# Second ranking placed behind the turns of its step, one product a block sooner, row copies on ScalarE, stores and first weights at other slots

## The chip, the cores and the metric

The kernel runs on one core of a Trainium2 chip. The core has five engines, each with its own instruction queue worked through in order: TensorE (PE, matmuls; its weight loads are shown apart as PEld), VectorE (DVE), ScalarE (ACT), GpSimd (POOL) and SyncE (SP), which here only issues transfers. They wait for one another through semaphores. Transfers between memory and the core are issued from SP or POOL and run on 16 DMA engines.

The metric is the device time of one launch in microseconds (us); smaller is better. Several runs are given by their median.

## The reference

Sigmoid attention for 8 batches of 12 heads, 448 tokens of width 64; its heads, put side by side, are rows of 768; then in each batch the 128 rows with the highest gate score go through a two-layer network and are added back.

```python
def _attn_ref(q, k, v):            # q, k, v: (8, 12, 448, 64)
    scores = 1.0 / np.sqrt(64) * np.matmul(q, k.transpose(0, 1, 3, 2)) - np.log(448)
    attn = 1.0 / (1.0 + np.exp(-scores))
    return np.matmul(attn, v)

def _moe_ref(x, w_gate, w1, w2, capacity):   # x: (8, 448, 768), w1: 768 x 1024, capacity 128
    scores = np.einsum('bsd,d->bs', x, w_gate)
    out = x.copy()
    for b in range(8):
        top_idx = np.argpartition(-scores[b], capacity)[:capacity]
        xe = x[b, top_idx]
        ye = np.maximum(xe @ w1, 0.0) @ w2
        g = 1.0 / (1.0 + np.exp(-scores[b, top_idx]))
        out[b, top_idx] = x[b, top_idx] + g[:, None] * ye
    return out
```

## The kernel before

**Steps and slots.** The heads are taken in 24 quads of four, two quads to a step: 12 steps `s`, of 7 slots `n` each. A batch is three quads. In a slot PE makes scores for a piece of the keys (`score`, L338) into the PSUM banks `PA`, ACT turns them into weights (`squash`, L352), and PE multiplies earlier weights with values (`value`, L367) into four output banks `PO`. Outputs of step s−1 are complete in slot 3 of step s. There DVE transposes them out (`takes`, L388) into the batch's tile `x_b`, of which there are two.

**Order by hand.** The whole program is one written order; each engine runs its share in that order. `slot(s, n)` issues the attention work and `after(s, n)` all else at that place. In slot 3 from step 4 on, `block(s)` adds work of the network, listed in `BLOCKS`: `("c", b)` chooses the rows of batch b, `("t", b)` turns the gathered rows, and `(m, p, key)` is product `key` of matrix m for the pair of batches p. Products are those of a seven-product scheme for two by two blocks: the two batches of a pair are combined, and so are quarters of the matrices, so the weights need sums of quarters.

**From output to chosen rows.** `gates` multiplies the outputs with the gate vector and adds up (L396, L399). When a batch is complete, `gate` forms its scores, and POOL writes them to memory (L424). `spread` reads them back onto all partitions as `rep` (L436, POOL queue). `ranking(b)` counts on DVE, in eight instructions over `rep` (L444, L447), how many tokens stand above each, and `place` makes a mask `hot` of it (L457, L459). `RANKED` gives the slot of each ranking: batch 0 at (3, 1), batch 1 at (4, 1). In a block, `choose(b)` takes the rows' numbers with small matmuls (L481 or L485) into a bank, `fetch` reads them from there on DVE (L492, L495), and POOL gathers the rows from memory (L505) into `xe`, one of three buffers. If the choice is the first item of a block, it stands ahead of the output transposes, and its fetch among them:

```python
        if work and work[0][0] == "c":
            chosen = choose(work[0][1], places.pop(0))
        takes(s - 1, 0)
        if work and work[0][0] == "c":
            fetch(*chosen)
            work = work[1:]
        takes(s - 1, 1)
```

**Turning and adding back.** `turn_rows` transposes the gathered rows on PE into two banks (L523). ACT copies the first half (L525), DVE the second (L526), for the products of the first matrix (`first`, L559). Products of the second (`second`, L623) are added into `xe` by DVE (`second_sums`, L634). After its last addition POOL scatters a batch's rows back (L643), which frees the row buffer.

**Weights.** Both matrices are loaded in quarters by SP, at the slots in `WEIGHTS` (L180). DVE makes sums of quarters (L207) at the slots in `MADE`; `KEPT` says when SP writes a sum to memory (L213), and `LENT` when it is read back (L241). Sums live in three spare tiles.

**SP's queue.** SP holds, in the written order, the loads of queries, keys (L104) and values (L153), the weights and sums, and the stores: `store` (L405) writes a quarter of a batch's rows in pieces of 128 bytes, four stores for each batch. A key load waits until DVE has turned the key tile before it (`turn`, L320); only one raw key tile exists. `FULL` is the step in whose slot 3 a batch is completed: 2, 3, 5, 6, 8, 9, 11, 12.

Of the kernel before, what the change touches and what calls it, by code (L numbers as in the profile page):

```python
# [12 lines left out]
ALU = mybir.AluOpType  # L13
# [4 lines left out]
def kernel(  # L18
# [90 lines left out]
    def spare(n):  # L109
        return spares.tile([P, QW], F32, name=f"spare{n}")  # L110
# [82 lines left out]
    def make_sum(m, key):  # L193
        if key == 5:
            room["a"] = spare(0)
        elif (m, key) == (1, 6):
            room["c"] = spare(2)
        elif m == 2 and key in (4, 6):
            room["d" if key == 4 else "c"] = spare(key // 4 if key == 4 else 0)
        a, b, c, d = [room.get(x) for x in "abcd"]  # L200
        w00, wx, w11 = [(w1_sb, w2_sb)[m - 1][:, x] for x in range(3)]
        dst, x, y, op = {
            (1, 5): (a, b, w11, ALU.add), (1, 7): (b, w00, b, ALU.subtract),
            (1, 6): (c, w11, b, ALU.subtract), (1, 3): (c, wx, c, ALU.subtract),
            (2, 5): (a, b, w00, ALU.subtract), (2, 7): (b, b, w11, ALU.subtract),
            (2, 6): (c, w00, b, ALU.subtract), (2, 4): (d, wx, c, ALU.subtract)}[m, key]
        nc.vector.tensor_tensor(out=dst, in0=x, in1=y, op=op)  # L207
        sums[m, key] = dst
        lent[m, key] = [dst[:, pr * QW // 2:(pr + 1) * QW // 2] for pr in range(2)]

    def keep_sum(m, key):
# [2 lines left out]
        sums[m, key] = t  # L214


    MADE = {(4, 4): (1, 5), (4, 5): (1, 7), (4, 6): (1, 6), (6, 4): (1, 3),
            (6, 6): (2, 5), (7, 0): (2, 7), (7, 4): (2, 6), (7, 5): (2, 4)}
    KEPT = {(4, 5): (1, 5), (4, 6): (1, 7), (5, 1): (1, 6), (6, 5): (1, 3),
            (7, 0): (2, 5), (7, 1): (2, 7), (7, 5): (2, 6), (7, 6): (2, 4)}  # L220
    WEIGHTS = {(2, 6): (1, 0), (3, 1): (1, 1), (3, 2): (1, 2), (3, 4): (1, None),
               (4, 1): (2, 0), (5, 1): (2, 1), (5, 2): (2, 2), (6, 4): (2, None)}

    def attn_tile(pr, n):
        return attnp.tile([P, 2, S], F32, name=f"attn{pr}_{n}")
# [285 lines left out]
    def turn_rows(b, both):  # L511


        n = CAP
        p, odd = divmod(b, 2)
        if not odd:
            t = moe.tile([P, 6 * KH * P], F32, name="rows_t")
            pairs[p] = {"x": t.rearrange("p (m k n) -> p m k n", m=6, k=KH)}
        x = pairs[p]["x"]
        ps = [t.rearrange("p (k n) -> p k n", n=P) for t in both]  # L520
        for t in range(KD):
            a, i = divmod(t, KH)
            nc.tensor.transpose(ps[a][:, i, :n], st[b]["xe"][:n, t * P:(t + 1) * P],  # L523
                                iden[:n, :n])
        nc.scalar.activation(x[:, 2 * odd, :, :n], ps[0][:, :KH, :n], AF.Copy)  # L525
        nc.vector.tensor_copy(x[:, 2 * odd + 1, :, :n], ps[1][:, :KH, :n])  # L526
        st[b]["gate"] = moe.tile([P, 1], F32, name="gate", bufs=4)
        nc.scalar.activation(st[b]["gate"][:n], st[b]["picked"][:n], AF.Sigmoid)
        if not odd:
            return  # L530
        for dst, y, z in ((4, 2, 0), (5, 3, 4), (2, 3, 2)):
            nc.vector.tensor_tensor(out=x[:, dst, :, :n], in0=x[:, y, :, :n],
                                    in1=x[:, z, :, :n], op=ALU.subtract)
        pairs[p]["turned"] = True
        last_row(p)
# [105 lines left out]
    def scatter(b):  # L641
# [37 lines left out]
    def block(s):  # L679

        places = [PA[1][:, 0], PO[0][0], PO[0][1], PA[0][:, 0], PO[1][0], PO[1][1], PA[0][:, 0]]
        work = BLOCKS.get(s, ())
# [4 lines that stand above are left out]
            fetch(*chosen)  # L687
            work = work[1:]
        takes(s - 1, 1)
        if s in FULL:  # L690
            gates(2 * s - 2)
        for item in work:
            if item[0] == "t":
                turn_rows(item[1], [places.pop(0) for _ in range(2)])
            elif item[0] == "c":
                fetch(*choose(item[1], places.pop(0)))
            else:
                finish(item, begin(item, places.pop(0)))
# [83 lines left out]
    def rest():  # L782
# [54 lines left out]
        for key in (1, 2, 6, 5, 3, 7, 4):  # L837
            do((2, p, key))

    def after(s, n):  # L840

        if n == NF and s:
            odd = s in FULL[1::2]
            if s > 4:
                load_v(s)
            if s in BLOCKS:
                block(s)
            elif s in FULL:
                gates(2 * s - 2)
            if odd and s > 3:  # L850
                gates(2 * s - 1)
            turn("q", 2 * s + 2)
            turn("k", 2 * s + 3)
            load("k", 2 * s + 4)
            turn("q", 2 * s + 3)
            if s not in FULL:
                gates(2 * s - 2)
            if not odd or s == 3:
                gates(2 * s - 1)
        for m, key, place in LENT.get((s, n), ()):  # L860
            lend(m, key, place)
        if s == 0:
            if n == 0:
                turn("k", 1)
                turn("q", 1)
                load("k", 2, 3)
                load("q", 2, 3)
            if n == 4:
                turn("k", 2, 3)
                load_v(1)  # L870
                load("k", 4)
            if n == 5:
                turn("q", 2, 3)
        if n == NF + 1 and 0 < s < 4:
            load_v(s + 1)
        if (s, n) in WEIGHTS:
            m, x = WEIGHTS[s, n]
            if x is None:
                load_left(m)
            else:  # L880
                load_held(m, x)
        if (s, n) in KEPT:
            keep_sum(*KEPT[s, n])
        if (s, n) in MADE:
            make_sum(*MADE[s, n])
        for b in range(B - 1):
            full = FULL[b]
            if (s, n) == ((4, 0) if b == 1 else (full, 5 + b % 2)):
                spread(b)
            for a, at in enumerate(((full, 5), (full, 6), (full + 1, 1), (full + 1, 2))):  # L890
                if (s, n) == (at if b < B - 2 else (full, 4 + a // 2)):
                    store(b, (a,))
            if (s, n) == RANKED[b]:
                ranking(b)

    RANKED = [(3, 1), (4, 1), (6, 1), (7, 5), (9, 1), (10, 5), (11, 6)]

    first_outs = ExitStack()

# [58 lines left out]
```

## Time and profile before

| | |
|---|---|
| median of 3 runs | 479.14 us (478.22 to 481.59) |
| profiled execution, its own time | 481.73 us |
| its span, from first to last instruction | 479.9 us |
| PE busy | 447.5 us, 93% |
| VectorE busy | 306.2 us, 64% |
| ScalarE busy | 188.2 us, 39% |
| GpSimd busy | 33.1 us, 7% |
| hardware DMA queue of SP | 67.97 MB, 55.7% of 16 engines |
| one slot of attention, squash to squash, undisturbed | 3.02 us |

The profile is of one execution. A row of a group or of a stretch of time gives line, engine, operation and tiles as output<-inputs. In a list in order of time the two first numbers are the start and the duration in us, and the bracket at the end is the idle time of the engine before the instruction and what ended it. A row of waits gives who waited, for whom, the total in us, how often and the longest. The row PEclk is the granted clock of PE in tenths of full speed, in 40 equal slices of the span; 9 is 90% or more.

### The profile page before, as it was taken

To read this page: it belongs to the slowest core of one execution; us is meant where nothing else is said; L and a number is where in the kernel's file an instruction comes from. 1 tells how busy PE (TensorE), PEld (TensorE's weight loads), DVE (VectorE), ACT (ScalarE), POOL (GpSimd) and SP (SyncE) were. 2 spreads that over 40 slices of the span, in tenths; PEclk is the share of its full clock that TensorE was granted. 3 is DMA by queue.
4 is the path that set the end of the run, shared out by engine and by line. 5 is a ranking of instruction groups with operands and counts; after the bars stand their busy time and mean duration, and the time that the engine had idled before them with its cause. 6 is when DMAs were issued, how large, how long until landed. Compare 5 with 4: busy or idle time off the path is not lost.

```text
span 479.9 us, 14338 instructions
## 1 busy us (share of the span) xinstructions
PE 447.5 (93%) x6374; PEld 267.4 (56%) x6374; DVE 306.2 (64%) x647; ACT 188.2 (39%) x249; POOL 33.1 (7%) x55
## 2 busy tenths in 40 slices
PE   8999997991997999999999599999999999999994
PEld 3556552441335549546556445854655756868952
DVE  4308195755936785865799377571695787886271
ACT  3776664661362462462362165156046250101000
POOL 6000010000001000100000300010000100101001
PEclk9999999997799999999999799999999999999999
DMA  8854318999898295189764378439894786711001
GB/s 231 239 156 110 125 17 171 285 222 243 200 319 237 66 196 107 36 240 289 192 222 117 102 213 188 96 63 280 191 296 135 152 194 162 126 41 72 1 0 66
DMA packets 112846, 76.80 MB, mean 160 GB/s; under 512 B 90304, under 2 KB 99136, under 8 KB 112784
## 3 DMA queue, kind: packets, MB, share of 16 engines
q1 hardware_dynamic: 110800, 67.97, 55.7%
q0 software_dynamic: 1984, 7.91, 5.8%
q8 instruction: 50, 0.82, 0.7%
q14 instruction: 12, 0.10, 0.1%
HBM read 55.41 MB, written 20.46 MB: 158 GB/s over the span
## 4 chain that ended last, share of the span: by engine, by line
PE 83%; DMA 6%; DVE 5%; issue 2%; ACT 2%; SPq 0%; POOLq 0%; DVEq 0%; ACTq 0%
PE a L338 27%; PE o L367 24%; PE o L623 10%; PE o L559 9%; PE a L559 7%; PE a L623 4%; DMA raw_k<-in_k_dram 1%; DMA rep<-scores 1%; ACT attn L352 1%; PE p L914 1%; DMA scores<-total 1%; DVE x_b L388 1%; DMA raw_v<-in_v_dram 1%; DMA xe<-out_dram,idx 1%; ACT hidden L352 1%
## 5 line engine op out<-in xcount | busy, mean ns | idle before, releaser
L338 PE MATMUL a<-qT,kT 32*64 32x448 f32 x2624 | 252.7, 546 | 14.0 <-DVE got L495 10.6
L352 ACT ACTIVATE attn<-a,bias_s 128x896 f32<-128x896 f32 x162 | 161.9, 1007 | 118.5 <-PE a L338 113.0
L367 PE MATMUL o<-attn,raw_v 32*64 32x448 f32 x2176 | 205.0, 546 | 0.7 <-DMA raw_v<-in_v_dram 0.4
L338 PEld LDWEIGHTS a<-qT,kT 32*64 32x64 f32 x2624 | 98.2, 133 | 106.7 <-ACT attn L352 53.8
L367 PEld LDWEIGHTS o<-attn,raw_v 32*64 32x64 f32 x2176 | 79.6, 133 | 38.3 <-issue 27.8
L388 DVE STREAM_TRANSPOSE x_b<-o 128x448 f32<-128x448 f32 x48 | 27.6, 622 | 54.9 <-PE o L367 42.9
L367 PE MATMUL o<-attn,rows_t 32*64 32x448 f32 x448 | 41.9, 537 | 0.0
L320 DVE STREAM_TRANSPOSE kT<-raw_k 128x448 f32<-128x448 f32 x42 | 24.2, 613 | 23.9 <-DMA raw_k<-in_k_dram 20.7
L575 ACT ACTIVATE hidden<-hidden 128x512 f32<-128x512 f32 x12 | 7.5, 630 | 68.5 <-DVE hidden L572 68.5
L399 DVE TENSOR_REDUCE gate_p<-scr 128x14 f32<-128x448 f32 x48 | 29.8, 621 | 1.7
L396 DVE TENSOR_TENSOR scr<-x_b,wg_b 128x448 f32<-128x448 f32 x48 | 29.3, 611 | 1.0
L559 PE MATMUL o<-rows_t,w_sb 128*128 128x128 f32 x192 | 24.4, 287 | 3.4 <-DVE rows_t L526 3.4
L623 PE MATMUL o<-w_sb,hidden 128*128 128x384 f32 x80 | 27.3, 486 | 0.0
L312 DVE STREAM_TRANSPOSE qT<-qT 128x896 f32<-128x896 f32 x23 | 25.0, 1088 | 2.8 <-DMA qT<-in_q_dram 2.7
L444 DVE TENSOR_SCALAR_CACHE_REDUCE scr<-rep,who 128x448 f32<-128x448 f32 (+1 forms) x32 | 21.5, 673 | 6.8 <-DMA rep<-scores 5.9
L559 PEld LDWEIGHTS o<-rows_t,w_sb 128*128 128x128 f32 x192 | 23.7, 203 | 3.8 <-DVE rows_t L526 3.6
L572 DVE TENSOR_TENSOR hidden<-o,hidden 128x512 f32<-128x512 f32 x19 | 12.6, 687 | 19.9 <-PE o L559 19.8
L634 DVE SCALAR_TENSOR_TENSOR xe<-o,gate,xe 128x384 f32<-128x384 f32 x34 | 19.5, 611 | 8.9 <-PE o L623 8.7
L447 DVE SCALAR_TENSOR_TENSOR scr<-rep,who,earlier 128x448 f32<-128x448 f32 (+1 forms) x32 | 21.9, 683 | 1.4
L525 ACT ACTIVATE rows_t<-o 128x384 f32<-128x384 f32 x7 | 3.4, 485 | 48.8 <-PE o L523 48.8
L367 PEld LDWEIGHTS o<-attn,rows_t 32*64 32x64 f32 x448 | 18.3, 131 | 5.2 <-issue 3.9
L559 PEld LDWEIGHTS a<-rows_t,spare 128*128 128x128 f32 x168 | 19.3, 192 | 3.2 <-ACT attn L352 3.2
(114 smaller groups left out, 398.2 us busy)
## 6 DMA issues: line engine op xcount, KB each, us to landing
qT<-in_q_dram SPq DMA_DIRECT2D x24, 448.0 KB, 5.5
out_dram<-x_b SPq DMA_DIRECT2D x32, 336.0 KB, 9.0
raw_k<-in_k_dram SPq DMA_DIRECT2D x22, 448.0 KB, 5.4
raw_v<-in_v_dram SPq DMA_DIRECT2D x36, 224.0 KB, 5.4
spare<-sum SPq DMA_DIRECT2D x18, 384.0 KB, 7.8
sum<-spare SPq DMA_DIRECT2D x8, 768.0 KB, 5.7
w_sb<-in_moe_w_dram SPq DMA_DIRECT2D x6, 768.0 KB, 10.7
rows_t<-in_v_dram SPq DMA_DIRECT2D x8, 224.0 KB, 7.9
```

The source lines that it names most:

```text
L312: nc.vector.transpose(heads["q", i], heads["q", i])
L320: nc.vector.transpose(kt[:, e], t[:, e].rearrange("p (a n) d -> p n a d", a=2))
L338: nc.tensor.matmul(out[y * Dh:(y + 1) * Dh, h % 2, :S], kt[d, e, r:r + 2].rearrange("d r t -> d (r t)"), qt[d, e], start=(e == 0), stop=(e ...
L352: nc.scalar.activation(a, psc[:, :, :S], AF.Sigmoid, bias=bias_s, scale=QK_SCALE)
L367: nc.tensor.matmul(PO[x][pr][j * Dh:(j + 1) * Dh, :S], raw_v[s][rows, 2 * pr + j, at:at + Dh], attn[s, pr, n][rows, j, :], start=((s, x, p ...
L388: nc.vector.transpose(x_tiles[b][:, :, 2 * g + pr, :], PO[x][pr][:, :S].rearrange("p (r t) -> p r t", t=TT))
L396: nc.vector.tensor_tensor(out=tmp, in0=x_tiles[b][:, :, hp, :], in1=wg_b[:, hp:hp + 1, :].to_broadcast([P, TB, TT]), op=ALU.mult)
L399: nc.vector.tensor_reduce(out=gate_parts[b][:, :, hp], in_=tmp, axis=AX.X, op=ALU.add)
L444: nc.vector.tensor_scalar(out=junk[:n], in0=rep[:n], scalar1=own, scalar2=0.0, op0=ALU.is_gt, op1=ALU.add, accum_out=above[:n, c:c + 1])
L447: nc.vector.scalar_tensor_tensor(out=junk[:n], in0=rep[:n], scalar=own, in1=earlier[:n, c, :], op0=ALU.is_equal, op1=ALU.mult, accum_out=l ...
L559: nc.tensor.matmul(ps[:, f, :n], w((t * FH + f) * P, P), x[:, t, :n], start=(t == 0), stop=(t == KH - 1))
L623: nc.tensor.matmul(ps[:n, :DH], h[:, t, :n], w(t * DH, DH), start=(t == 0), stop=(t == FH - 1))
```

## The change

Six edits:

- The ranking of batch 1 leaves slot (4, 1) and stands in slot 3 of step 4, behind the output transposes and the turns of queries and keys, ahead of the gate work.
- Product 6 of the second matrix for the first pair, (2, 0, 6), goes from the head of block 8 to block 7, and (2, 0, 7) from block 7 to block 8. The sums of the second matrix are made in another order for it, with the same count of instructions and in two spare tiles.
- The second half of the turned rows is copied by ScalarE (`activation` with Copy), as the first half is.
- The four loads of the first matrix go from (2, 6), (3, 1), (3, 2), (3, 4) to (1, 2), (1, 5), (2, 1), (2, 2). Three of the four loads of the second go from (4, 1), (5, 1) and (5, 2) to (5, 1), (5, 5) and (6, 1).
- Three sums of the first matrix are made one step later, at (5, 4) to (5, 6), and written to memory at (6, 0) and (6, 1).
- The four stores of a batch go from (full, 5), (full, 6), (full+1, 1), (full+1, 2) to (full, 3), (full, 5), (full+1, 0), (full+1, 1). For batch 6 they go from two at (11, 4) and two at (11, 5) to (11, 3), two at (11, 4) and (11, 5). In slot 3 the store stands right behind the output transposes, ahead of the load of the next keys.

```diff
@@ make_sum
-        elif m == 2 and key in (4, 6):
-            room["d" if key == 4 else "c"] = spare(key // 4 if key == 4 else 0)
-        a, b, c, d = [room.get(x) for x in "abcd"]
+        elif (m, key) == (2, 7):
+            room["c"] = spare(0)
+        a, b, c = [room.get(x) for x in "abc"]
...
-            (2, 5): (a, b, w00, ALU.subtract), (2, 7): (b, b, w11, ALU.subtract),
-            (2, 6): (c, w00, b, ALU.subtract), (2, 4): (d, wx, c, ALU.subtract)}[m, key]
+            (2, 5): (a, b, w00, ALU.subtract), (2, 6): (b, w11, a, ALU.subtract),
+            (2, 7): (c, w00, b, ALU.subtract), (2, 4): (b, wx, b, ALU.subtract)}[m, key]
...
-    MADE = {(4, 4): (1, 5), (4, 5): (1, 7), (4, 6): (1, 6), (6, 4): (1, 3),
-            (6, 6): (2, 5), (7, 0): (2, 7), (7, 4): (2, 6), (7, 5): (2, 4)}
-    KEPT = {(4, 5): (1, 5), (4, 6): (1, 7), (5, 1): (1, 6), (6, 5): (1, 3),
-            (7, 0): (2, 5), (7, 1): (2, 7), (7, 5): (2, 6), (7, 6): (2, 4)}
-    WEIGHTS = {(2, 6): (1, 0), (3, 1): (1, 1), (3, 2): (1, 2), (3, 4): (1, None),
-               (4, 1): (2, 0), (5, 1): (2, 1), (5, 2): (2, 2), (6, 4): (2, None)}
+    MADE = {(5, 4): (1, 5), (5, 5): (1, 7), (5, 6): (1, 6), (6, 4): (1, 3),
+            (6, 6): (2, 5), (7, 0): (2, 6), (7, 4): (2, 7), (7, 5): (2, 4)}
+    KEPT = {(6, 0): [(1, 5), (1, 7)], (6, 1): [(1, 6)], (6, 5): [(1, 3)],
+            (7, 0): [(2, 5)], (7, 1): [(2, 6)], (7, 5): [(2, 7)], (7, 6): [(2, 4)]}
+    WEIGHTS = {(1, 2): (1, 0), (1, 5): (1, 1), (2, 1): (1, 2), (2, 2): (1, None),
+               (5, 1): (2, 0), (5, 5): (2, 1), (6, 1): (2, 2), (6, 4): (2, None)}
@@ turn_rows
-        nc.vector.tensor_copy(x[:, 2 * odd + 1, :, :n], ps[1][:, :KH, :n])
+        nc.scalar.activation(x[:, 2 * odd + 1, :, :n], ps[1][:, :KH, :n], AF.Copy)
@@ BLOCKS
-        7: [(1, 0, 3), (2, 0, 2), (2, 0, 5), (2, 0, 7), (2, 0, 3), ("t", 2)],
-        8: [(2, 0, 6), ("c", 3), (2, 0, 4), (1, 1, 1), (1, 1, 2), ("t", 3)],
+        7: [(1, 0, 3), (2, 0, 2), (2, 0, 5), (2, 0, 6), (2, 0, 3), ("t", 2)],
+        8: [("c", 3), (2, 0, 4), (2, 0, 7), (1, 1, 1), (1, 1, 2), ("t", 3)],
@@ block, behind the second takes
         takes(s - 1, 1)
+        stores(s, NF)
@@ ahead of after
+    FIRST = 4
+
+    def stores(s, n):
+
+        for b in range(B - 1):
+            full = FULL[b]
+            for a, at in enumerate(((full, 3), (full, 5), (full + 1, 0), (full + 1, 1))):
+                if (s, n) == (at if full < NS - 1 else (full, 3 + (a + 1) // 2)):
+                    store(b, (a,))
@@ after
-            elif s in FULL:
-                gates(2 * s - 2)
+            else:
+                stores(s, n)
+                if s in FULL:
+                    gates(2 * s - 2)
...
             if s not in FULL:
                 gates(2 * s - 2)
+            if s == FIRST:
+                ranking(1)
...
-            for a, at in enumerate(((full, 5), (full, 6), (full + 1, 1), (full + 1, 2))):
-                if (s, n) == (at if b < B - 2 else (full, 4 + a // 2)):
-                    store(b, (a,))
             if (s, n) == RANKED[b]:
                 ranking(b)
-
-    RANKED = [(3, 1), (4, 1), (6, 1), (7, 5), (9, 1), (10, 5), (11, 6)]
+        if n != NF:
+            stores(s, n)
+
+    RANKED = [(3, 1), None, (6, 1), (7, 5), (9, 1), (10, 5), (11, 6)]
```

More of the change, by code (lines that the diff above doesn't have):

```diff
@@ L881, in after @@
                 load_held(m, x)
-        if (s, n) in KEPT:
-            keep_sum(*KEPT[s, n])
+        for m, key in KEPT.get((s, n), ()):
+            keep_sum(m, key)
         if (s, n) in MADE:
```

## The prediction

> **What bounds the kernel now.** I read the page's busy times first, then who TensorE (PE) waited for, then each long wait in order of time on the engines that take part, then the clock.
>
> ```profile
> PE 447.5 (93%) x6374; PEld 267.4 (56%) x6374; DVE 306.2 (64%) x647; ACT 188.2 (39%) x249; POOL 33.1 (7%) x55
> PEclk9999999997799999999999799999999999999999
> ```
>
> PE is the bound: 32.4 of 479.9 us without a matmul. No other engine is near full, but the clock row has dips at 108 to 132 us and near 270. PE's waits, longest first:
>
> ```profile
> PE a L338 <- DVE got L495: 10.6, 1, 10.6
> PE o L523 <- DMA xe<-out_dram,idx: 5.1, 1, 5.1
> PE o L559 <- DVE rows_t L526: 3.4, 1, 3.4
> PE a L338 <- issue: 2.9, 1, 2.9
> ```
>
> Four single waits make 22 of the 32 us; the rest is start and tail. Between them a slot of attention takes a steady 3.02 us from squash to squash. What stands on VectorE (DVE) in the first wait, in step 4:
>
> ```profile
> 105.77 1.17 DVE L320 STREAM_TRANSPOSE kT<-raw_k 128x448 f32<-128x448 f32 x2 [4.41 <-DMA raw_k<-in_k_dram]
> 112.85 0.68 DVE L444 TENSOR_SCALAR_CACHE_REDUCE scr<-rep,who 128x448 f32<-128x448 f32 x1 [5.91 <-DMA rep<-scores]
> ...
> 118.91 0.69 DVE L459 TENSOR_TENSOR hot<-slots,place_s 128x512 f32<-128x512 f32 x1
> 119.52 1.17 DVE L388 STREAM_TRANSPOSE x_b<-o 128x448 f32<-128x448 f32 x2
> 120.62 0.12 DVE L492 TENSOR_SCALAR idx<-a 128x1 int32<-128x1 f32 x1
> ```
>
> PE is ready for the block at 109.2 (first choosing product, L485). DVE stands at the second ranking: it waits until 112.85 for the spread scores, ranks until 119.5, and only then empties the output banks (L388) and frees the score bank (L492, L495). Nothing in this block needs that ranking. The second wait is on GpSimd's (POOL) queue in block 8:
>
> ```profile
> 264.36 1.03 POOL L643 DMA_INDIRECT out_dram<-xe,idx  x1 [1.08 <-DVE xe L634]
> 268.23 0.99 POOL L505 DMA_INDIRECT xe<-out_dram,idx  x1 [2.84 <-DVE hidden L572]
> ```
>
> The gather of batch 3 goes out at 268.23, after the scatter of batch 0 (landed 267.44). They share a row buffer: there are three. The third is in block 5, and what each idle stretch does to the clock shows in the windows after it (columns: PE, PEld, DVE, ACT, POOL busy; granted clock; DMA share; GB/s):
>
> ```profile
> 154.15 4.54 PE L559 MATMUL o<-rows_t,w_sb 128*128 128x128 f32 x24 [3.38 <-DVE rows_t L526]
> ```
>
> ```profile
> 121.00:127.00 6.00, 6.00 (x72) 2.26 (x80) 5.90 (x10) 1.01 (x1) 1.05 (x1) 0.52 1.21 270
> 154.20:157.50 3.30, 3.30 (x15) 3.30 (x16) 0.00 (x0) 0.00 (x0) 0.27 (x1) 0.50 0.07 24
> 272.20:277.00 4.80, 4.80 (x46) 2.52 (x54) 3.23 (x6) 0.58 (x2) 1.60 (x2) 0.50 0.45 119
> ```
>
> After each of the three, PE resumes at half clock.
>
> **Ranking of batch 1 behind the turns of step 4.** Eight comparing instructions of 0.68 with short reads, and two to place, from 112.85 to 119.5: 6.7 us, plus the wait before them, move behind the output transposes and three turns. What is late next in that block is the ordinary order of a block: two transposes of 0.62, then L492 and L495, before the score bank is free, about 1.2 us of PE idle (in block 5 the same four end 1.4 us after its choosing products start). Gain in idle time 10.6 − 1.2 = 9.4. The half clock goes too: granted from 113.1 to 126.8, PE working from 120.9, so 5.9 us at half, 2.95 lost. Together 12.3 us.
>
> Does DVE have room? After the outputs (done about 112) it has 3.3 of turns, 6.7 of ranking, 5.2 of gates (four pairs of 0.63 + 0.62) and 1.2 of the key turn of step 5: free near 129. Block 5's outputs are ready seven slots of 3.02 after the block, about 132. The scores may land as late as 118 before this costs anything; before they landed at 112.7, behind weights that are now elsewhere. Cost nothing; without that 3 us of cover, one for one.
>
> [...] By the rows it is 2.95, 1.7 (154.15 to 157.5) and 2.4 (272.2 to 277.0), 7.05 us, 1.5% of the span. I take the rows.
>
> **Rows copied by ScalarE (ACT).** In block 5 the second half of batch 0's rows (L526, DVE) stood behind the gate work until 153.5, while ACT was idle from 147.9 to 150.8. On ACT both copies take 0.49 each, one after the other, ready at about 148; product (1,0,1) ends at 150.5, so (1,0,2) follows at once. Gain 3.4 + 1.7 of clock = 5.1. Next late is the first rows' turn of batch 1: its gather is issued at 147.5, a gather lands 5.1 us later by the median, so 152.6, and PE wants it at 153.2: nothing to 1 us. ACT's two copies of batch 1 stand behind a relu that waits for DVE: at most 0.3 us. I take 5.0. In the six other blocks or tail places the copy moves 0.56 us from DVE to 0.49 on ACT in series; PE's next matmuls write other banks first. Nothing, at most 0.3 each.
>
> **Sixth product in block 7.** Batch 0 gets its last addition from (2,0,3) in block 7, so its scatter leaves some 20 us before the gather of batch 3, which moves to the head of block 8 and lands under four products (10.7 us by 2.68). The wait of 5.1 and the clock's 2.4 go: 7.5. Block 11 has the same members in the same order as the new block 8 and takes 16.0 us from squash to squash against 23.1 (279.65 − 256.51) now. That is 7.1, which I take. Blocks 7 and 10 get equal; the same five products as before, so nothing.
>
> **First weights and stores.** The four loads of the first matrix go to steps 1 and 2. DMA is 28% busy from 48 to 72 us; the loads need about 2.0 to 2.9 us each by the landings of such loads in a full queue. The keys behind them are turned 12 to 18 us after their issue: hidden. Above it lies PE's own instruction fetch: the 2.9 of "issue" starts at 78 together with one. A new one could cost 0 to 3; that old one has the same keys, values and a store queued ahead, so I leave it. The stores keep number and size. Each goes one slot or so sooner; on SP the first of each batch waits for the block's output transposes, with the key load behind it, but that load itself waits for a later DVE turn. One store adds 1.9 to 3.4 us to what lands behind it; the keys have 12 us. Nothing, bounds −1 to +2.
>
> **The sums of the first matrix, a step later.** Three DVE instructions of 1.75 (5.3 us) leave step 4 and stand in step 5, ahead of a key turn and the third ranking:
>
> ```profile
> 168.62 1.17 DVE L320 STREAM_TRANSPOSE kT<-raw_k 128x448 f32<-128x448 f32 x2 [0.42 <-PE a L338]
> ...
> 178.07 1.12 DVE L472 SCALAR_TENSOR_TENSOR sums<-hot,who,sums 128x128 f32<-128x128 f32 x3
> 181.32 2.24 DVE L388 STREAM_TRANSPOSE x_b<-o 128x448 f32<-128x448 f32 x4 [2.13 <-PE o L367]
> ```
>
> DVE had 2.1 + 0.4 idle, so block 6's outputs come 2.8 us late. Its first product (2.7 us) goes to a bank that waits for nothing, the second needs the first output bank: 2.8 + 0.6 − 2.7 = 0.7 us. Their three writes to memory and two loads of the second matrix now stand on SP ahead of step 6's values. From their marginal landings (2 us, 2 to 3 with a store) I put the last value near 196 on before's clock; PE wants it at 195 to 196.7. I take 0 and 2 as bounds, 0.5 as value.
>
> **Sum.** 12.3 + 5.0 + 7.1 − 0.7 − 0.5 = 23.2 us. The profiled execution of before took 481.73 (span 479.9 and 1.8 around it) and would take 458.5. It lies 2.6 above the median of the runs, 479.14; against that median the forecast is 455.9, so 456.
>
> **Rivals.** (1) The work moved comes back as waits: DVE late at blocks 5 and 6 and the values late at block 6. For it: only 2 to 3 us of slack at each. Against: each is bounded by 3. Stalls of 3, 3 and 2 and 2 of half clock take 10 back: 466.
> (2) More goes: the "issue" wait vanishes with the weights gone from 73 to 100 us, and its slot drops from 6.9 to 3.1: 3.8 more, 452; if the four slots of steps 7 and 10 that take 3.6 to 3.8 also came down to 3.02, 2.9 more, 449.
> (3) The change does less than it says: the gather of batch 3 still late, since scatter and stores of its memory must land first. Against: they are 20 us earlier. Then 23.2 − 7.1, 463.
> (4) Slower: loads for attention starve. Place: step 6, where values are queued behind three sums, two weight loads and four stores, 20 us of transfers. Each us that they land after block 6 stalls PE, and the next steps' keys follow. It decides only if values land over 23 us late, at about 219; DMA was nearly idle from 189 to 204 (13% busy from 192), so the backlog would drain. At 30 late, 455.9 + 30 makes 486.
>
> **Chances.** The forecast 0.74 (450 to 461), rival 1 0.11, rival 2 0.07, rival 3 0.04, rival 4 0.04. About 1% is what a measurement of this kernel can tell from no change. Faster by more: 0.93; within: 0.03; slower: 0.04. The range takes the forecast's own, most of rival 2 and a part of 1 and 3: 449 to 464.
>
> **What would show it.** L495 no more among PE's waits, or under 1.5 us; ranking lines L444 behind two L312 in step 4; no clock of 0.5 after 100 us until the tail. L526 on ACT and the two products of block 5 without gap. POOL's scatter far ahead of the gather of batch 3, block 8 at 16 us. New: up to 1 us before the second product of block 6. Wrong if PE waits on "raw_v" at block 6 or on a key's turn, or if instruction waits appear in steps 1 and 2.

## The result, and the profile after

The changed kernel takes 456.90 us (median of four runs, 455.50 to 459.74), the kernel before 479.22 us (four runs, 478.22 to 481.59). The ratio is 0.954, 95% interval 0.949 to 0.959: faster by 22.3 us. 456 was forecast.

The profiled execution took 459.74 us (span 457.9), the longest of the four: 2.8 above their median. It stands against a span of 479.9, so its ledger has 22.0 us to account for.

The head of the page of after, and its row of the granted clock:

```profile
PE 442.5 (97%) x6374; PEld 266.2 (58%) x6374; DVE 302.2 (66%) x639; ACT 191.2 (42%) x257; POOL 33.1 (7%) x55
...
PEclk9999999899999999999999999999999999999998
```

PE's time without a matmul fell from 32.4 to 15.4 us, and its busy time by 5.0 with the same 6,374 matmuls. Of this second part about 3.6 is the clock: PE worked 14.1 us at half clock before and 6.8 after, and half of such time is lost: in before a group of four score matmuls (L338) began every 0.75 us at 0.50 (121.7 to 125.4) and every 0.38 at 1.00 (127.2 to 128.4). The other 1.4 isn't placed. The dips at 108 to 132 and near 270 us are gone; one near 85 is new. PE's waits, longest first:

```profile
PE a L338 <- issue: 2.9, 1, 2.9
PE o L367 <- issue: 1.7, 2, 1.4
PE p L928 <- DVE bias_s L922: 1.5, 1, 1.5
PE o L559 <- DVE x_b L388: 0.9, 2, 0.7
...
PE a L338 <- DVE got L495: 0.5, 1, 0.5
```

The waits of 10.6, 5.1 and 3.4 us are no longer there. What has come is the second row: PE waits for no data there ("issue"); the text calls this an instruction wait, and the last section shows why. VectorE in step 4, where the wait of 10.6 was:

```profile
114.86 1.18 DVE L388 STREAM_TRANSPOSE x_b<-o 128x448 f32<-128x448 f32 x2 [8.71 <-ACT attn L352]
116.00 0.14 DVE L495 COPY got<-a 128x1 f32<-128x1 f32 x1
119.20 1.07 DVE L312 STREAM_TRANSPOSE qT<-qT 128x896 f32<-128x896 f32 x1
...
122.78 0.68 DVE L444 TENSOR_SCALAR_CACHE_REDUCE scr<-rep,who 128x448 f32<-128x448 f32 x1
...
128.77 0.69 DVE L459 TENSOR_TENSOR hot<-slots,place_s 128x512 f32<-128x512 f32 x1
```

The bank is free at 116.1 and the ranking begins 6.6 us later, behind outputs and turns. VectorE even stood idle for 8.7 us ahead of the outputs. PE in block 5, in order of time:

```profile
140.24 2.94 PE L559 MATMUL a<-rows_t,w_sb 128*128 128x128 f32 x24
143.03 2.84 PE L559 MATMUL o<-rows_t,w_sb 128*128 128x128 f32 x24
145.95 0.52 PE L523 MATMUL o<-iden,xe 128*128 128x128 f32 x3
```

The second product follows the first, and the turn of batch 1's rows follows the second without a gap: the gather landed in time. POOL's queue around block 8:

```profile
221.52 1.03 POOL L643 DMA_INDIRECT out_dram<-xe,idx  x1 [27.54 <-DVE xe L634]
...
245.54 0.99 POOL L505 DMA_INDIRECT xe<-out_dram,idx  x1 [22.99 <-DVE got L495]
```

The scatter now leaves 24 us before the gather that needs its row buffer, instead of 3.9.

Since a wait can hide in a busy PE, I also compared the time from each squash (L352) to the next, slot by slot. These slots changed; together they make 22.1 us:

| slot | before, us | after, us | difference |
|---|---|---|---|
| (4, 4), block 4 | 18.33 | 5.27 | −13.06 |
| (5, 4), block 5 | 17.17 | 12.54 | −4.63 |
| (8, 4), block 8 | 23.14 | 16.29 | −6.85 |
| (10, 2) and (10, 4), block 10 | 23.99 | 20.58 | −3.41 |
| (4, 0) and (7, 4) | 21.89 | 21.23 | −0.66 |
| (1, 0), (2, 1), (2, 2) | 9.49 | 14.00 | +4.51 |
| (3, 2) | 6.91 | 8.08 | +1.17 |
| (6, 4) and (11, 4) | 34.26 | 35.05 | +0.79 |

The three blocks of the forecast are there at their sizes. The two rows below them are not what was forecast: block 10 gained, and steps 1 to 3 lost. The windows of the loss (columns: start and end, length, then busy time of PE, PEld, DVE, ACT, POOL; granted clock; DMA share; GB/s):

```profile
52.70:54.10 1.40, 0.02 (x4) 0.02 (x4) 0.00 (x0) 0.00 (x0) 0.00 (x0) 1.00 1.04 399
55.20:58.60 3.40, 3.40 (x44) 2.20 (x36) 0.00 (x0) 1.59 (x2) 0.00 (x0) 0.50 1.04 388
82.40:85.40 3.00, 0.10 (x1) 0.00 (x0) 2.75 (x8) 0.28 (x4) 0.00 (x0) 1.00 1.06 166
85.90:89.30 3.40, 3.40 (x46) 1.21 (x30) 3.09 (x10) 0.90 (x1) 0.00 (x0) 0.50 0.74 240
```

The pattern appears twice: PE stands still for 1.4 or 2.9 us while all 16 DMA engines are busy (share 1.04 and 1.06), and soon after works 3.4 us at half clock (0.50).

### The profile page after: what moved, and what is told of

It reads as the page before. It is cut to its first block, busy times and chain, and to the rows that moved or that the text cites. A ratio compares the mean times of both kernels' runs of the same rounds, so it can differ in the third digit from the quotient of the medians.

```text
span 457.9 us, 14344 instructions
## 1 busy us (share of the span) xinstructions
PE 442.5 (97%) x6374; PEld 266.2 (58%) x6374; DVE 302.2 (66%) x639; ACT 191.2 (42%) x257; POOL 33.1 (7%) x55
## 3 DMA queue, kind: packets, MB, share of 16 engines
q1 hardware_dynamic: 110800, 67.97, 58.6%
## 4 chain that ended last, share of the span: by engine, by line
PE 90%; DVE 3%; ACT 3%; issue 2%; DMA 1%; POOLq 0%; ACTq 0%; DVEq 0%
PE a L338 30%; PE o L367 26%; PE o L623 11%; PE o L559 9%; PE a L559 7%; PE a L623 3%; ACT attn L352 2%; PE p L928 1%; ACT hidden L352 1%; DMA out_dram<-xe,idx 1%; DVE x_b L388 1%; PE o L523 1%; DVE scr L447 1%; DVE scr L444 1%; PE a L523 1%
## 5 line engine op out<-in xcount | busy, mean ns | idle before, releaser
L338 PE MATMUL a<-qT,kT 32*64 32x448 f32 x2624 | 249.0, 543 | 3.7 <-issue 2.9
L352 ACT ACTIVATE attn<-a,bias_s 128x896 f32<-128x896 f32 x162 | 161.9, 1007 | 103.2 <-PE a L338 99.3
L367 PE MATMUL o<-attn,raw_v 32*64 32x448 f32 x2176 | 200.1, 540 | 0.4 <-issue 0.3
L338 PEld LDWEIGHTS a<-qT,kT 32*64 32x64 f32 x2624 | 96.4, 132 | 98.9 <-ACT attn L352 53.6
L367 PEld LDWEIGHTS o<-attn,raw_v 32*64 32x64 f32 x2176 | 78.0, 132 | 30.2 <-issue 21.0
L367 PE MATMUL o<-attn,rows_t 32*64 32x448 f32 x448 | 44.0, 560 | 1.4 <-issue 1.4
L634 DVE SCALAR_TENSOR_TENSOR xe<-o,gate,xe 128x384 f32<-128x384 f32 x36 | 20.5, 612 | 8.8 <-PE o L623 8.7
L559 PE MATMUL o<-rows_t,w_sb 128*128 128x128 f32 x192 | 22.7, 275 | 0.0
L559 PEld LDWEIGHTS o<-rows_t,w_sb 128*128 128x128 f32 x192 | 22.2, 192 | 0.3
```

Source lines behind the costliest of these rows:

```text
L338: nc.tensor.matmul(out[y * Dh:(y + 1) * Dh, h % 2, :S], kt[d, e, r:r + 2].rearrange("d r t -> d (r t)"), qt[d, e], start=(e == 0), stop=(e ...
L352: nc.scalar.activation(a, psc[:, :, :S], AF.Sigmoid, bias=bias_s, scale=QK_SCALE)
L367: nc.tensor.matmul(PO[x][pr][j * Dh:(j + 1) * Dh, :S], raw_v[s][rows, 2 * pr + j, at:at + Dh], attn[s, pr, n][rows, j, :], start=((s, x, p ...
L559: nc.tensor.matmul(ps[:, f, :n], w((t * FH + f) * P, P), x[:, t, :n], start=(t == 0), stop=(t == KH - 1))
```

## The experiments

The total being right doesn't say that its terms were. Two readings stood against each other. One is the forecast's: each part has its own price, read from the place where it acts, and the weights and stores are worth nothing. The other is that the parts hold each other up: with 12 us fewer waits in step 4 the same transfers have to land in less time, so that the ranking and the copies would pay only once the weights are out of the queue of steps 3 to 5. Five kernels take one part alone; four take two parts together or leave one out of the full change; three test what was then left over. All compute the whole result. The times that follow are medians, each against the kernel before on the same chip, with the 95% interval of the ratio.

**The ranking alone.**

```diff
             if s not in FULL:
                 gates(2 * s - 2)
+            if s == 4:
+                ranking(1)
...
-    RANKED = [(3, 1), (4, 1), (6, 1), (7, 5), (9, 1), (10, 5), (11, 6)]
+    RANKED = [(3, 1), None, (6, 1), (7, 5), (9, 1), (10, 5), (11, 6)]
```

> Before, with only the second ranking moved behind the turns of step 4; the three sums of the first matrix stay in step 4. If the wait of 10.6 us and its half clock go and DVE has cover: 12 to 13 us less than before, about 466. If DVE's room in step 4 decides (ranking 6.7 and sums 5.3 both between blocks 4 and 5), block 5 finds its outputs 2 to 3 us late: 9 to 11 us less, about 469, and a wait for L388 or L495 at block 5. If the ranking's wait was hidden by another one: under 5 us less.

484.61 us against 480.42, ratio 1.007 (1.003 to 1.012): slightly slower, and outside all that was written down for it. Slot (4, 4) fell from 18.33 to 5.28 us as in the full change, and then slot (5, 0) rose from 3.02 to 8.84 and slot (5, 4) from 17.17 to 25.95: +14.6 against −13.05. PE's waits from 115 to 166 us in this kernel:

```profile
PE o L367 <- DMA raw_v<-in_v_dram: 3.5, 1, 3.5
PE a L338 <- DVE qT L312: 3.0, 2, 2.6
PE o L523 <- DVE x_b L388: 2.9, 1, 2.9
PE o L559 <- DVE rows_t L526: 2.2, 1, 2.2
```

What is late next can be followed back on VectorE of the same kernel, in order of time:

```profile
118.60 1.11 DVE L312 STREAM_TRANSPOSE qT<-qT 128x896 f32<-128x896 f32 x1 [7.39 <-DMA qT<-in_q_dram]
...
125.87 0.68 DVE L444 TENSOR_SCALAR_CACHE_REDUCE scr<-rep,who 128x448 f32<-128x448 f32 x1
...
136.76 3.55 DVE L207 TENSOR_TENSOR spare<-w_sb,spare 128x1536 f32<-128x1536 f32 x2
...
141.31 1.14 DVE L388 STREAM_TRANSPOSE x_b<-o 128x448 f32<-128x448 f32 x2
```

VectorE waits 7.39 us for the queries of step 5, so turns, ranking and the sums of the first matrix all stand later than PE wants them, and the outputs of block 5 are taken at 141.3. In the full change the same queries landed at 110.8 and 113.1, where VectorE turns them at 119.2; here they landed at 118.6 and 119.7. The values of step 5 took as long, in both kernels the times from issue to landing of that tile's loads:

```profile
DMA to landing us min/median/max: 14.0/14.2/14.4
```

```profile
DMA to landing us min/median/max: 4.0/4.8/5.4
```

The first is this kernel, the second the full change; before had a median of 8.0. The stall wasn't removed, it moved one step on.

**The copy alone.**

```diff
-        nc.vector.tensor_copy(x[:, 2 * odd + 1, :, :n], ps[1][:, :KH, :n])
+        nc.scalar.activation(x[:, 2 * odd + 1, :, :n], ps[1][:, :KH, :n], AF.Copy)
```

> Before, with only the second half of the turned rows copied by ScalarE. By the prediction's step: 5 us less, 474, with block 5 at 12.2 to 12.6 us from squash to squash instead of 17.2. If the gather of batch 1 or the relu ahead of the copies is late next: 1 to 3 us less.

479.08 against 480.42, ratio 0.998 (0.994 to 1.002): no difference. PE in block 5 of this kernel:

```profile
146.42 2.84 PE L559 MATMUL o<-rows_t,w_sb 128*128 128x128 f32 x24
...
152.11 0.65 PE L523 MATMUL o<-iden,xe 128*128 128x128 f32 x3 [2.85 <-DMA xe<-out_dram,idx]
```

The wait for L526 went, and 2.85 us for the gather of batch 1 took its place. It was issued at 143.29 and landed at 151.97: 8.7 us, where the prediction had put 5.1 from the median of all gathers. The slot went from 17.17 to 16.62 us.

**Product 6 in block 7 alone.** The edit is that of the change: the two lines of `BLOCKS` and the order of the second matrix's sums.

```diff
-        7: [(1, 0, 3), (2, 0, 2), (2, 0, 5), (2, 0, 7), (2, 0, 3), ("t", 2)],
-        8: [(2, 0, 6), ("c", 3), (2, 0, 4), (1, 1, 1), (1, 1, 2), ("t", 3)],
+        7: [(1, 0, 3), (2, 0, 2), (2, 0, 5), (2, 0, 6), (2, 0, 3), ("t", 2)],
+        8: [("c", 3), (2, 0, 4), (2, 0, 7), (1, 1, 1), (1, 1, 2), ("t", 3)],
```

> Before, with only product (2, 0, 6) in block 7 and (2, 0, 7) in block 8, and the sums of the second matrix made in that order. By the prediction's step: 7 us less, 472, block 8 at 16.0 to 16.3 instead of 23.1, block 7 unchanged within 0.5. If the gather of batch 3 is late for another reason than the shared row buffer (stores, the choosing): under 3 us less.

471.91 against 480.42, ratio 0.982 (0.974 to 0.991). Slot (8, 4) went from 23.14 to 16.01 us: 7.1, as worked out. This part needs no other.

**The stores alone.** The edit is the function `stores` of the change and its three calls, with nothing else.

```diff
         takes(s - 1, 1)
+        stores(s, NF)
...
-            for a, at in enumerate(((full, 5), (full, 6), (full + 1, 1), (full + 1, 2))):
-                if (s, n) == (at if b < B - 2 else (full, 4 + a // 2)):
-                    store(b, (a,))
...
+        if n != NF:
+            stores(s, n)
```

> Before, with only the stores at their new slots. By the prediction (stores cost and give nothing): no change within 1 us. By what the profile of the change shows in step 10: the values of step 10 are issued sooner, slots (10, 2) and (10, 4) take 0.5 and 2.9 us less, 3 to 3.5 us less in all, 476. If the gain in step 10 comes from another part: no change there.

474.99 against 480.42, ratio 0.989 (0.985 to 0.993): a gain where nothing was forecast. Slot (10, 4) falls from 20.43 to 17.56 us. The waits of the kernel before at that place, 343 to 356 us, with the weight loads of PE:

```profile
PEld o L367 <- DMA raw_v<-in_v_dram: 1.7, 2, 1.2
PE o L367 <- DMA raw_v<-in_v_dram: 0.4, 1, 0.4
```

PE itself waits 0.4 us there, and so the list of its waits shows nothing; the weight loads that it needs next wait 1.7. The values of step 10 landed between 349.6 and 353.1, and the attention slot behind the block wanted the first at 348.8. With the stores ahead of them by a slot, they are in time. The six kernels with the new stores all have 17.56 in this slot, the eight with the old ones 18.72 to 20.43. So against most executions the stores give 1.2 to 1.8 us here, and against the profiled execution of before 2.9. The medians say more, 5.4; a part of it lies in slot (4, 4), which came out 2.6 us shorter here, but 4.0 shorter in the kernel with the copy alone, and so is no evidence for the stores.

**The weights and sums alone.**

```diff
-    MADE = {(4, 4): (1, 5), (4, 5): (1, 7), (4, 6): (1, 6), (6, 4): (1, 3),
+    MADE = {(5, 4): (1, 5), (5, 5): (1, 7), (5, 6): (1, 6), (6, 4): (1, 3),
...
-    WEIGHTS = {(2, 6): (1, 0), (3, 1): (1, 1), (3, 2): (1, 2), (3, 4): (1, None),
-               (4, 1): (2, 0), (5, 1): (2, 1), (5, 2): (2, 2), (6, 4): (2, None)}
+    WEIGHTS = {(1, 2): (1, 0), (1, 5): (1, 1), (2, 1): (1, 2), (2, 2): (1, None),
+               (5, 1): (2, 0), (5, 5): (2, 1), (6, 1): (2, 2), (6, 4): (2, None)}
```

> Before, with only the weight loads, the sums of the first matrix and their writes at their new slots. By the prediction these moves give nothing and cost about 1 us: 479 to 481. If the transfer queue in steps 3 to 5 is what makes scores, queries and gathers late: the spread scores land some us sooner, the wait in step 4 shrinks by 2 to 6 us, and an instruction wait near slot (2, 1) takes up to 4 of it back: 475 to 480.

482.17 against 479.39, ratio 1.008 (1.003 to 1.013): slightly slower, above both ranges that were written down. Slot (2, 1) rose from 3.21 to 7.09 us: an instruction wait of 1.4, then half clock from 53.2 to 56.6, as in the full change. Block 4 kept a wait of 8.4 us for the ranking. Alone, this part only costs.

**The change without the weights and sums.** This takes the full change and sets `MADE`, `KEPT` and `WEIGHTS` of the first matrix, and the loads of the second, back to the slots of before.

```diff
-    MADE = {(5, 4): (1, 5), (5, 5): (1, 7), (5, 6): (1, 6), (6, 4): (1, 3),
+    MADE = {(4, 4): (1, 5), (4, 5): (1, 7), (4, 6): (1, 6), (6, 4): (1, 3),
...
-    WEIGHTS = {(1, 2): (1, 0), (1, 5): (1, 1), (2, 1): (1, 2), (2, 2): (1, None),
-               (5, 1): (2, 0), (5, 5): (2, 1), (6, 1): (2, 2), (6, 4): (2, None)}
+    WEIGHTS = {(2, 6): (1, 0), (3, 1): (1, 1), (3, 2): (1, 2), (3, 4): (1, None),
+               (4, 1): (2, 0), (5, 1): (2, 1), (5, 2): (2, 2), (6, 4): (2, None)}
```

> The changed kernel with weight loads, sums of the first matrix and their writes back at the old slots; the other five edits stay. If the parts simply add: the waits of steps 1 and 2 (4 to 5 us) and of block 6 (0.5) go, 452. If the queue decides: waits for the turned queries at (5, 0), for the gathered rows and for the values in block 5 come back, 3 to 14 us in all: 460 to 470.

471.68 against 479.39, ratio 0.984 (0.976 to 0.991), some 15 us behind the full change (0.954). PE's longest waits:

```profile
PE o L367 <- DMA raw_v<-in_v_dram: 4.3, 1, 4.3
PE o L523 <- DVE x_b L388: 2.9, 1, 2.9
PE a L338 <- DVE qT L312: 2.5, 2, 2.3
```

They are those of the ranking alone, at the same places: slot (5, 0) takes 8.41 us and slot (5, 4) 25.33. So the part that is slightly slower by itself is worth 15 us in the company of the others.

**The ranking with the weights and sums.** Both edits above on the kernel before, without the other three parts.

```diff
+            if s == 4:
+                ranking(1)
...
-    WEIGHTS = {(2, 6): (1, 0), (3, 1): (1, 1), (3, 2): (1, 2), (3, 4): (1, None),
+    WEIGHTS = {(1, 2): (1, 0), (1, 5): (1, 1), (2, 1): (1, 2), (2, 2): (1, None),
```

> Before, with the second ranking moved and the weight loads and sums at their new slots; stores, copies and product as before. If the ranking moved alone gained nothing because the queue was full with weights and sums: now most of the 13 us of block 4 stay gained, less up to 4 at slot (2, 1): 465 to 470, and (5, 0) is back at 3.0. If the stores (two at a time) are what fills it: waits at (5, 0) or block 5 remain, 473 to 480.

468.59 against 479.39, ratio 0.978 (0.968 to 0.987). One part costs 4.2 us alone and the other 2.8, and both together gain 10.8. Slot (5, 0) is back at 3.02 us, slot (4, 4) is at 5.10, and the long waits left are the two that the other parts take away:

```profile
PE o L523 <- DMA xe<-out_dram,idx: 5.2, 1, 5.2
PE o L559 <- DVE rows_t L526: 3.4, 1, 3.4
```

**The change without the new stores.** This is the full change with the four stores of a batch back at the slots of before.

```diff
-        stores(s, NF)
...
+            for a, at in enumerate(((full, 5), (full, 6), (full + 1, 1), (full + 1, 2))):
+                if (s, n) == (at if b < B - 2 else (full, 4 + a // 2)):
+                    store(b, (a,))
```

> The changed kernel with the stores back at their old slots. If the parts add: the values of step 10 are late again by 2.9 and (10, 2) by 0.5, 460. If the stores also make room around step 4: a further 2 to 6 us at (5, 0) or block 5, 462 to 466.

461.19 against 479.39, ratio 0.963 (0.956 to 0.970), about 4 us behind the full change by the medians. Slot (10, 4) takes 18.89 us in place of 17.56, slot (10, 2) 3.83 in place of 3.02, and in block 5 the gather comes 2.6 us late (slot 14.75 in place of 12.54). These make 4.35. The two intervals overlap, so that 4 us is not a sharp number; the profiled execution of this kernel was even 2 us shorter than that of the full change, because slots (2, 1) and (3, 2), with their instruction waits, took 5.2 us less in it.

**The weights sooner still.** The instruction waits of the full change stand where the DMA engines are full (share 1.04 and 1.06 in the windows above). If they come from the queue, they should go with the loads:

```diff
-    WEIGHTS = {(1, 2): (1, 0), (1, 5): (1, 1), (2, 1): (1, 2), (2, 2): (1, None),
+    WEIGHTS = {(1, 0): (1, 0), (1, 1): (1, 1), (1, 2): (1, 2), (1, 5): (1, None),
```

> The changed kernel with the four loads of the first matrix at (1, 0), (1, 1), (1, 2) and (1, 5), three of them in the idle stretch from 35 to 42 us. If the instruction wait near (2, 1) comes from the weights queued with the values and queries of step 2: no such wait, slot (2, 1) at 3.2 to 4, and 0 to 4 us less than the changed kernel, 453 to 457. If it comes from somewhere else: as the changed kernel, 455 to 460.

454.64 against 479.94, ratio 0.948 (0.944 to 0.952). Slot (2, 1) has an instruction wait of 0.3 us in place of 1.4, and takes 4.34 us in place of 6.66. But with the load slots of the full change this slot took anything from 3.24 to 7.09 us in six kernels, so one profile doesn't show that the move did it. In slot (3, 2) an instruction wait of 1.6 us stays, with half clock behind it (0.993 granted over the whole run, 0.996 in the version that follows).

**Sooner, and the values of step 3 ahead of its keys.** On top of the last edit:

```diff
+            if s == 2:
+                load_v(3)
...
-        if n == NF + 1 and 0 < s < 4:
+        if n == NF + 1 and s in (1, 3):
             load_v(s + 1)
```

> As e7_weights_sooner, and the values of step 3 are loaded ahead of the waiting key load in slot 3 of step 2 instead of behind it. If the instruction wait at (3, 2) (2.9 us in the profiles of before and of the change, 1.2 to 1.7 in others) comes from the transfers queued at once behind that key load: slot (3, 2) at 3.0 to 3.8 instead of 5.2 to 8.1, and 1.5 to 5 us less than e7: 450 to 455. If not: as e7.

453.70 against 479.94, ratio 0.946 (0.942 to 0.950). Slot (3, 2), which took 5.2 to 8.1 us in every other kernel, takes 3.13, and no half clock shows before the tail: its PEclk row has 9 in all slices but the last. PE's longest wait:

```profile
PE o L523 <- DMA xe<-out_dram,idx: 1.5, 1, 1.5
```

No instruction wait over 0.2 us is left; 1.1 us came back in slot (3, 4), and the gather of block 5 is 1.5 us late. This is the fastest version that was run. By medians it lies 3.2 us ahead of the changed kernel; the intervals of the two ratios (0.942 to 0.950, and 0.949 to 0.959) overlap by a hair, so that it is likely, and not certain, that it beats it. Against the version before it, it gains 0.9 us by medians, inside the spread of either.

**The sums back in steps 4 and 5, the loads still early.** This separates the two halves of the weights part:

```diff
-    MADE = {(5, 4): (1, 5), (5, 5): (1, 7), (5, 6): (1, 6), (6, 4): (1, 3),
+    MADE = {(4, 4): (1, 5), (4, 5): (1, 7), (4, 6): (1, 6), (6, 4): (1, 3),
...
-    KEPT = {(6, 0): [(1, 5), (1, 7)], (6, 1): [(1, 6)], (6, 5): [(1, 3)],
+    KEPT = {(4, 5): [(1, 5)], (4, 6): [(1, 7)], (5, 1): [(1, 6)], (6, 5): [(1, 3)],
```

> The changed kernel with only the three sums of the first matrix and their writes back in steps 4 and 5; the loads stay early. If the loads in steps 3 to 5 are what made the queue late: as the changed kernel within 1 %, 454 to 460. If the sums are (5.3 us of DVE between ranking and block 5, 2.4 MB of writes ahead of the values): DVE 2 to 3 us late at block 5 and the values late, 460 to 466.

460.18 against 479.94, ratio 0.959 (0.953 to 0.965), 3.3 us behind the full change by the medians, with intervals that overlap. Block 5 is where it shows: slot (5, 4) takes 19.80 us in place of 12.54, with half clock from 144.8 to 151.6 behind these two waits:

```profile
PE o L523 <- DMA xe<-out_dram,idx: 1.7, 1, 1.7
...
PE o L367 <- DMA raw_v<-in_v_dram: 1.5, 1, 1.5
```

The values took 11.0 to 12.3 us from issue to landing, 4.0 to 5.4 in the full change, and no wait for VectorE stands there. Slot (5, 0) stays at 3.02. So the early loads of the weights bring the queries of step 5 in time, and the later sums, with their three writes to memory, bring the gather and the values of block 5 in time.

**The copy with the weights and sums.** The second pair, on the kernel before:

```diff
-        nc.vector.tensor_copy(x[:, 2 * odd + 1, :, :n], ps[1][:, :KH, :n])
+        nc.scalar.activation(x[:, 2 * odd + 1, :, :n], ps[1][:, :KH, :n], AF.Copy)
...
-    WEIGHTS = {(2, 6): (1, 0), (3, 1): (1, 1), (3, 2): (1, 2), (3, 4): (1, None),
+    WEIGHTS = {(1, 2): (1, 0), (1, 5): (1, 1), (2, 1): (1, 2), (2, 2): (1, None),
```

> Before, with the copies on ScalarE and the weight loads and sums at their new slots. The copy alone left block 5 at 16.6 because the gather of batch 1 landed late. If the weights and sums were what held that gather back: block 5 at 12.0 to 13.5 us, and 475 to 478, 4 to 5 less than the weights alone (482.2). If not: block 5 above 15.5, 480 to 483.

477.62 against 479.94, ratio 0.995 (0.992 to 0.998). Slot (5, 4) takes 12.61 us, 4.6 less than before; with the copy alone it was 0.6 less, and with the weights alone it took 18.59. The gather's 8.7 us from issue to landing are 5.5 here. So the copy, too, pays only with a clear queue.

The slots of the profiled executions beside one another:

| kernel | (2, 1) | (4, 4) | (5, 0) | (5, 4) | (8, 4) | (10, 4) |
|---|---|---|---|---|---|---|
| before | 3.21 | 18.33 | 3.02 | 17.17 | 23.14 | 20.43 |
| ranking alone | 3.07 | 5.28 | 8.84 | 25.95 | 23.06 | 18.72 |
| copy alone | 3.24 | 14.33 | 3.02 | 16.62 | 23.08 | 19.36 |
| weights alone | 7.09 | 15.15 | 3.02 | 18.59 | 23.12 | 19.10 |
| ranking, weights | 3.24 | 5.10 | 3.02 | 15.61 | 23.08 | 19.08 |
| copy, weights | 5.29 | 15.33 | 3.02 | 12.61 | 22.43 | 18.98 |
| change, no weights | 3.02 | 5.28 | 8.41 | 25.33 | 16.29 | 17.56 |
| full change | 6.66 | 5.27 | 3.02 | 12.54 | 16.29 | 17.56 |

It shows also how far one profile may be trusted: slot (4, 4) takes 18.33 us in before and 14.33 in the kernel with the copy alone, whose edit acts only behind that slot. The profile of before was at the long end there, and the gain worked out from it with it.

## Why the prediction was right

The total was right to 1 us, and four of its terms were right at their places. It was right with one statement in it that the runs refute, and to be right to 1 us took luck: kernels whose edits don't reach slot (4, 4) show 14.3 to 18.3 us there, and two terms that were left out nearly cancel.

**Ranking of batch 1 behind the turns of step 4: 12.3 us, measured 13.1.** The mechanism is as told; against the 14.3 us that the slot takes in the kernel with the copy alone, the same edit would measure 9.1. The wait put in its place was too large: 1.2 us assumed for the ordinary order of a block, 0.45 in the trace. The granted clock stays at full speed behind the block (1.00 from 108 to 130). Of the 13.06 us of the slot, 10.6 − 0.45 are the wait, and the other 2.9 the half clock: the 2.95 taken from the rows. "Cost nothing" for VectorE's room held: the ranking ended at 129.5, and the outputs were taken at 138.4, after an idle time. It held because the queries had landed, which is the next point.

**First weights and stores: "Nothing, bounds −1 to +2".** This is the step that failed, in two ways.

The stores gain 1.7 to 3.4 us in step 10 by the slots (1.2 to 2.9 in the block's slot and 0.5 in slot (10, 2)), and 5.4 by the medians of the run with them alone (3.6 to 7.1 by the interval), against a bound of 1 us of gain. It was missed because PE's waits show 0.4 us there: the values' trickle is hidden in a PE that the profile counts as busy, and shows in its weight loads, with 1.7.

For the weights, the step had asked what the loads cost at their new place, and not what their going does at the old one. The cost was within its bound or somewhat over it: "A new one could cost 0 to 3", and slot (2, 1) shows 0 to 3.9 us over six kernels with the same load slots there, 3.4 in the profiled execution of after, because half clock follows the 1.4 us of waiting (0.50 from 55.2 to 58.6). The worth is 15 us: full change 456.9, without the weights 471.7. It doesn't stand as a term of the sum; it is what the terms of blocks 4 and 5 rest on. The prediction did see that the scores landed late "behind weights that are now elsewhere", and gave it only 3 us of cover. It should have asked of the queries, keys, values and the gather of step 5 where they land when PE comes 13 us sooner and the queue is as it was. The kernel with the ranking alone gives the answer: 14.6 us of new waits for 13.05 taken away.

That the sum came out is not luck in the whole: the change as priced did move the weights, and the sum silently took for granted what that brings. But the same working, applied to the ranking alone, would have forecast a gain of 12 us for a kernel that is slightly slower.

**Rows copied by ScalarE: 5.0, measured 4.6.** Again under the same condition: 0.6 with the queue as it was. "Nothing to 1 us" for the gather was taken from the median of all gathers (5.1); in block 5 of the kernel with the copy alone it took 8.7.

**Sixth product in block 7: 7.1, measured 6.8, and 7.1 alone.** This term needs no other, as the run of it alone shows.

**The sums of the first matrix, a step later: −0.7 and −0.5, measured −0.5 in block 6** (slot (6, 4), 18.25 to 18.74). The values of step 6 were in time: no wait for them is in the list. What the step left out is its gain: with the sums back, block 5 takes 7.3 us more.

**The rivals.** Rival 4, loads that starve attention, was placed in step 6 and decides nothing there; its mechanism, values and queries late behind other transfers, is what the kernels without the weights part show, in step 5. Rival 2 was wrong in its cause: with the weights gone the wait of slot (3, 2) stayed (8.08 us after, 6.91 before). It went when the values of step 3 were loaded earlier too, for 3.8 us in that slot. Rival 1 came as a sign only: 0.5 us in block 6. Rival 3 is refuted, since scatter and gather lie 24 us apart and block 8 takes 16.3 us.

**What would show it.** Right: L495 at 0.5 us, the ranking behind the turns, two products without a gap, block 8 at 16.3 us, no half clock after 100 us until the tail. But one sign that was named for being wrong came too: an instruction wait in step 2, 1.4 us in slot (2, 1).

**The sum, set right for this execution**: 13.1 + 4.6 + 6.8 + 3.4 (block 10) + 0.7 (small slots) − 4.5 (steps 1 and 2) − 1.2 (slot (3, 2)) − 0.8 (blocks 6 and 11) = 22.1, against 22.0 of the spans; 23.2 was forecast. The gain of the stores and the cost of the early weights nearly cancel, which is why their being left out didn't show in the total.

What stays open: why the instructions that PE waits for come late. That the transfers ahead hold them up is inferred from the waits' going when loads are moved. And the profiles of kernels that are the same up to that point differ by 2.5 us in slot (2, 1) and by 1.7 in slot (3, 2), so that a difference of that size in one profile isn't a cause yet.

## What to carry to other kernels

Before a stall's length is booked as gain, move everything behind it forward by that length and ask of each load in the following steps whether it still lands in time: the transfers stay as many, and have less time. Parts that share a queue are priced together, since a part that is neutral or slower alone may be what lets the others pay. And waits for loads that trickled in behind a busy PE were hardly in the list of its waits here (0.4 us, and 1.7 in that of its weight loads): compare the steady slots one by one, and read the waits of the weight loads too.

## What was not expected of the hardware

**The clock.** Half clock followed some short idle times as well. In the changed kernel PE stood for 1.4 us (52.7 to 54.1) and was granted 0.50 from 55.2 to 58.6; the kernels with the weights alone (1.4 us, then 53.2 to 56.6), with the copy alone (1.4, then 230.9 to 234.3) and with ranking and weights (1.3, then 219.4 to 222.8) show the same. But 1.4 us in the same slot gave no half clock in the kernels with the sums back and with copy and weights, and 2.9 us in slot (3, 2) gave none in before (77.9 to 80.8, then 1.00 to 85) and some in after (82.5 to 85.4, then 0.50 from 85.9 to 89.3).

The long stalls of before came with longer stretches at 0.50: 13.7 us with the stall of 10.6 (113.1 to 126.8, PE at work in 5.9 of them), 6.8 with that of 5.1 (270.2 to 277.0, at work in 4.8), 3.4 with that of 3.4 (154.1 to 157.5, at work nearly throughout). What decides whether half clock follows a short wait, and how long it stays, is not shown: no run moved a wait by itself.

**The instructions.** The trace also holds the packets that bring instructions: each page counts 50 of them on q8, 0.82 MB, which is one of 16 KB for about 255 of PE's 12,748 matmuls and weight loads. In before and in the changed kernel PE has three waits on "issue" of over 1 us. They stand at two places of its program, in slots (2, 1) and (3, 2), and each ends 1.5 us after such a packet has landed: in before one landed at 79.3, and PE went on at 80.8; in the changed kernel they landed at 52.6 and 83.9, and PE went on at 54.1 and 85.4. At the first place the packet began to move when PE had 6 instructions left up to the stop; in before, which doesn't stop there, the same packet began when it had 108 left. At the second place it began, in both kernels, 0.6 to 0.7 us after PE had started the last one ahead of the stop. So PE did wait for its instructions in these traces.

**The issue of a store.** Some issues took long, and what is behind them in SP's order was then late. In before the second of two stores issued in a row took SP from 105.1 to 112.5, 7.4 us, and the query load behind it was issued only then, at 112.95; in the changed kernel one took from 110.2 to 114.9, 4.7 us. The first store of each pair, of the same size and in the same pieces, took 0.6 us. That a full queue makes the difference is inferred: the DMA share was 1.06 and 1.01 in the long issues, 1.13 and 0.84 in the short ones. What is shown is that a store held up what stands behind it by its issue, besides its own transfer.
